# Linear attention and a gated feed-forward on one core: a new order of all steps

## The chip, the cores and the metric

The kernel runs on one core of a Trainium2 chip. The metric is device time in microseconds of one execution; lower is better. Before the change the median of three runs is 251.77 us (251.26 to 253.02).

## What is computed

The reference, cut to what matters:

```python
# q, k, v: 8 batches x 8 heads x 576 rows x 64, float32
phi = lambda x: np.where(x > 0, x, np.exp(x) - 1.0) + 1.0
kv  = einsum('bhsd,bhse->bhde', phi(k), v)
z   = sum(phi(k), axis=2)
x   = einsum('bhsd,bhde->bhse', phi(q), kv) / (einsum('bhsd,bhd->bhs', phi(q), z) + 1e-6)
x   = x.transpose(0, 2, 1, 3).reshape(4608, 512)
out = (((x @ w1) * (x @ w2)) @ w3) @ w_out        # w1, w2: 512x1024, w3: 1024x1024, w_out: 1024x512
```

## The kernel before

The kernel is a set of small steps (functions marked `@step`) and one string, ORDER, that lists every call of them. The scheduling is manual: each engine executes its own instructions in the order in which the string issues them, and an instruction that waits holds up everything behind it on its engine. A word such as `x:q,3,4,4` calls the step x with the arguments q, 3, 4, 4. A second string, GATES, adds waits between transfers: several of the loads on SP may not issue before the load of q of batch 1 has landed.

Of each batch, 512 of the 576 rows are worked on as one chunk of four row blocks (numbers 0 to 7); the remaining 64 rows of all batches together make a ninth chunk, number 8. Weights: `w3 @ w_out` is first multiplied out to `wf_sb` (steps w3t, w3c, wa, wf, wc), so that each chunk needs two matmul stages.

The steps, with their lines in the kernel before:

- Loads: `ld` (L119) brings one batch of q, k or v, 1 MB; `lr` and `lp` (L127, L135) the 64 rest rows of one batch or of two; `lw`, `lo`, `l3` (L144, L151, L159) the weights, cast to bf16, on POOL's queue. The last argument names the queue: s for SP, g for POOL. Loads of a 1 MB kind share five buffers.
- phi: `x` (L166, ACT) takes the exponential, `t` (L172, DVE) max and add, `m` (L180, DVE) the minimum of the two; `xr`, `tr`, `mr` (L194 to L212) do so for the rest rows. There is one buffer for the phi of q and one for that of k.
- `v` and `vr` (L217, L225) cast v to bf16, on DVE or ACT as the argument v or a says. There is one buffer for v.
- `kv` (L238, batches 0 and 1) and `kk` (L254, batches 2 to 7) multiply phi(k) by v on PE. `kc`, `kh`, `kg` copy the result from PSUM to `kvb`.
- phi(q) is transposed by PE (`qt`, copy `qc`) in batches 0 and 1, by a DMA on SP (`qd`, L299) after that.
- `na` (L311, PE) multiplies by kvb, `nd` (L317 to L319, three DVE instructions) divides and writes x; `qdr`, `nar`, `ndr` do so for the rest rows.
- x is transposed by PE (`xp`, L353, copy `xc`, L358) in batches 0 to 2, by a DMA on SP (`xd`, L363) in batches 3 to 7; `xdr` (L368) is that of the rest rows.
- `f` (L420, PE) makes one 128-row slice of x@w1 and x@w2, two PSUM banks of four matmuls each; `ac` (L434, ACT) copies the first to SBUF and `ab` (L439, DVE) multiplies. `fk` is a part of an f.
- `o` (L445, PE) makes one block of the output, `oc` (L451) copies it, `st` (L463) stores it. `ol` (L472 to L476) does so in two column halves on two engines and two queues.
- `warm` (L113) are matmuls on zeros.

PSUM has two pools: four banks shared by f, o, qt, xp, w3t and wf, and two pairs of banks shared by kv, kk, na, nar and wa. A new f therefore waits until the f two before it has been read by its ac and its ab.

Of the kernel before, what the change touches and what calls it, by code (L numbers as in the profile page):

```python
# [18 lines left out]
def kernel(  # L19
# [11 lines left out]
    nc = tc.nc  # L31
    B, H, S, D = q.shape
# [4 lines left out]
    NJ = 4  # L37
    R = S - NJ * P
    W = NJ * D
    E1 = D + 1  # L40
# [6 lines left out]
    ld = ctx.enter_context(tc.tile_pool(name="ld", bufs=5))  # L47
# [18 lines left out]
    vts = [wpool.tile([P, NJ, H, E1], BF16, name=f"vt{i}") for i in range(1)]  # L66
    vrz = wpool.tile([P, 2, H, E1], BF16)
# [179 lines left out]
    @step  # L247
    def kk(b, hp):
        o = got(ps, ("kk", b), at_ps, [P, 2, 512], F32, "at", "kvp")[:, 0]
        kj, kr, vt = ph["k", b], ph["kr", b // 2, 2], vts[b % len(vts)]  # L250
        for j in range(NJ + 1):
            for u in range(2):
                h = 2 * hp + u
                nc.tensor.matmul(o[u * D:(u + 1) * D, hp * E1:(hp + 1) * E1],  # L254
                                 kj[:, hp, j, u] if j < NJ else kr[:, h * D:(h + 1) * D],
                                 vt[:, j, h] if j < NJ else vrz[:, b % 2, h],
                                 start=(j == 0), stop=(j == NJ))
# [233 lines left out]
    xc:0,1,a xc:0,0,a ld:v,1,4,4,g fk:0,0,0,2 wc:6,v xp:0,2 xp:0,3 xc:0,2,a xc:0,3,v fk:0,0,2,1
    fk:0,0,3,1 ac:0,0,a ab:0,0 f:0,2 ac:0,2,a f:0,3 xr:k,0,1 tr:k,0,1 ab:0,2 ac:0,3,a mr:k,0,1 wf:7
    ab:0,3 f:0,5 wc:7,a vr:1,v ac:0,5,a f:0,7 ab:0,5 x:k,1,0,4 t:k,1,0,4 t:k,1,4,4 f:0,6 ac:0,7,a
    m:k,1,0,1 x:k,1,4,4 ab:0,7 m:k,1,0,0 ac:0,6,a m:k,1,4,2 f:0,4 m:k,1,4,3 x:q,1,4,4 lp:v,1,s t:q,1,0,4
    ab:0,6 ac:0,4,a ld:v,2,0,8,s f:0,1 x:q,1,0,4 t:q,1,4,4 ab:0,4 v:1,0,4,a m:q,1,0,1 m:q,1,4,2
    v:1,6,2,a m:q,1,4,3 kv:1,0 m:q,1,0,0 kv:1,1 ac:0,1,a lp:k,1,s kv:1,3 v:1,4,2,v kc:1,0,1,1,a qt:1,2,2
    kc:1,0,1,0,v kh:1,3,1,a kh:1,3,0,v ab:0,1 qt:1,0,2 qc:1,2,2,a kv:1,2 qc:1,0,2,v o:0,0 kh:1,2,0,a
    ld:k,2,0,8,s kh:1,2,1,a na:1,2 oc:0,0,a na:1,0 o:0,2 nd:1,2 st:0,0,g ld:q,2,0,8,s v:2,4,4,a vr:2,v
    nd:1,0 vr:3,a xp:1,2 na:1,1 oc:0,2,v v:2,0,4,a xp:1,0 na:1,3 nd:1,1 o:0,1 st:0,2,g xc:1,0,a
    ld:v,3,0,8,s nd:1,3 xc:1,2,a xp:1,1 oc:0,1,v xp:1,3 o:0,3 xc:1,1,a tr:k,1,2 st:0,1,g xr:k,1,2  # L500
    xc:1,3,a mr:k,1,2 x:k,2,4,4 t:k,2,0,4 f:1,7 lp:k,2,s t:k,2,4,4 oc:0,3,a m:k,2,4,2 ac:1,7,a m:k,2,4,3
    st:0,3,g x:k,2,0,4 ab:1,7 f:1,0 m:k,2,0,1 m:k,2,0,0 ac:1,0,a t:q,2,0,4 x:q,2,0,4 f:1,4 ab:1,0
    x:q,2,4,4 ld:q,3,0,8,s t:q,2,4,4 m:q,2,0,0 ac:1,4,a m:q,2,0,1 f:1,6 m:q,2,4,2 m:q,2,4,3 ab:1,4
    ac:1,6,a qd:2 f:1,2 ab:1,6 ac:1,2,a ab:1,2 f:1,1 ac:1,1,a f:1,3 x:q,3,4,4 t:q,3,0,4 lp:v,2,s ab:1,1
    ac:1,3,a tr:k,2,2 xr:k,2,2 t:q,3,4,4 f:1,5 ld:k,3,0,8,s x:q,3,0,4 ab:1,3 mr:k,2,2 ac:1,5,a kk:2,0
    kk:2,1 kk:2,2 kk:2,3 v:3,0,4,v ld:q,4,0,8,s ab:1,5 o:1,1 kg:2,0,a kg:2,1,a v:3,4,4,v m:q,3,0,0
    m:q,3,4,3 na:2,2 m:q,3,0,1 oc:1,1,a na:2,0 o:1,3 m:q,3,4,2 nd:2,0 st:1,1,g qd:3 nd:2,2 xp:2,0
    oc:1,3,a o:1,0 t:k,3,4,4 vr:4,a st:1,3,g t:k,3,0,4 x:k,3,4,4 xp:2,2 x:k,3,0,4 na:2,3 m:k,3,4,2
    na:2,1 m:k,3,4,3 o:1,2 nd:2,3 oc:1,0,a xc:2,2,a st:1,0,g m:k,3,0,0 xc:2,0,a nd:2,1 xp:2,3 x:q,4,0,4
    m:k,3,0,1 xp:2,1 t:q,4,0,4 xc:2,3,a kk:3,0 kk:3,1 kk:3,2 kk:3,3 oc:1,2,v xc:2,1,a ld:v,4,0,8,s  # L510
    kg:3,0,v st:1,2,g x:q,4,4,4 kg:3,1,v f:2,0 vr:5,v t:q,4,4,4 ac:2,0,a f:2,1 ab:2,0 ac:2,1,a m:q,4,4,2
    m:q,4,0,0 na:3,0 m:q,4,0,1 na:3,2 f:2,6 ab:2,1 nd:3,2 ac:2,6,a nd:3,0 f:2,4 v:4,4,4,a v:4,0,4,v
    ab:2,6 ac:2,4,a na:3,3 m:q,4,4,3 ld:k,4,0,8,s na:3,1 ab:2,4 f:2,7 lp:k,3,s nd:3,3 ac:2,7,a nd:3,1
    qd:4 f:2,3 ab:2,7 ac:2,3,a f:2,2 ab:2,3 ac:2,2,a t:k,4,0,4 x:k,4,4,4 f:2,5 t:k,4,4,4 x:k,4,0,4
    ab:2,2 ld:k,5,0,8,s xd:3 m:k,4,4,2 ac:2,5,a m:k,4,4,3 m:k,4,0,0 ab:2,5 o:2,2 m:k,4,0,1 xr:k,3,2
    tr:k,3,2 mr:k,3,2 oc:2,2,a kk:4,0 kk:4,1 kk:4,2 kk:4,3 o:2,3 kg:4,0,a st:2,2,g kg:4,1,a na:4,0
    oc:2,3,a na:4,3 o:2,1 nd:4,0 x:k,5,0,4 st:2,3,g nd:4,3 ld:q,5,0,8,s x:k,5,4,4 t:k,5,4,4 na:4,1
    na:4,2 oc:2,1,a o:2,0 nd:4,1 st:2,1,g m:k,5,4,2 nd:4,2 ld:v,5,0,8,s oc:2,0,a t:k,5,0,4 xd:4 st:2,0,g
    m:k,5,0,1 m:k,5,4,3 m:k,5,0,0 f:3,7 ac:3,7,a f:3,2 ab:3,7 ac:3,2,a x:q,5,4,4 t:q,5,0,4 f:3,4 ab:3,2
    x:q,5,0,4 t:q,5,4,4 f:3,3 m:q,5,4,2 ac:3,4,a m:q,5,0,1 ab:3,4 ac:3,3,a lp:v,3,s m:q,5,4,3 v:5,4,4,a  # L520
    m:q,5,0,0 f:3,0 ab:3,3 v:5,0,4,a qd:5 ac:3,0,a ab:3,0 kk:5,0 kk:5,1 kk:5,2 kk:5,3 f:3,6 kg:5,0,a
    kg:5,1,v ac:3,6,a ld:v,6,0,8,s f:4,6 ab:3,6 ac:4,6,a f:4,7 ab:4,6 vr:6,a vr:7,v ac:4,7,a f:4,3
    ab:4,7 ac:4,3,a na:5,2 na:5,0 ab:4,3 f:4,0 nd:5,2 v:6,0,4,a v:6,4,4,v ac:4,0,a lp:q,0,s na:5,3
    nd:5,0 f:4,4 ab:4,0 ld:q,6,0,8,s ac:4,4,a nd:5,3 ld:k,6,0,8,s f:4,1 ab:4,4 ac:4,1,a f:4,2
    ld:v,7,0,8,s ab:4,1 ac:4,2,a f:4,5 ab:4,2 x:q,6,4,4 t:q,6,4,4 t:q,6,0,4 x:q,6,0,4 f:3,1 m:q,6,4,2
    m:q,6,4,3 ac:4,5,a m:q,6,0,0 m:q,6,0,1 ac:3,1,a ab:4,5 o:4,0 qd:6 x:k,6,4,4 ab:3,1 t:k,6,0,4
    x:k,6,0,4 o:4,3 t:k,6,4,4 oc:4,0,a tr:q,0,2 xr:q,0,2 m:k,6,4,2 st:4,0,g m:k,6,4,3 ld:k,7,0,8,s
    m:k,6,0,1 oc:4,3,v o:4,2 mr:q,0,2 st:4,3,g m:k,6,0,0 oc:4,2,v qdr:0 kk:6,0 kk:6,1 kk:6,2 kk:6,3
    v:7,0,4,a o:4,1 st:4,2,g kg:6,1,v v:7,4,4,v kg:6,0,v na:5,1 oc:4,1,v f:3,5 nd:5,1 st:4,1,g ac:3,5,a
    xd:5 na:6,0 na:6,3 ab:3,5 o:3,1 nd:6,3 nd:6,0 o:3,3 oc:3,1,v x:k,7,0,4 t:k,7,4,4 st:3,1,g  # L530
    ld:q,7,0,8,s x:k,7,4,4 t:k,7,0,4 o:3,0 m:k,7,0,1 oc:3,3,a m:k,7,0,0 m:k,7,4,2 st:3,3,g m:k,7,4,3
    oc:3,0,a st:3,0,g kk:7,0 kk:7,1 kk:7,2 kk:7,3 o:3,2 kg:7,1,v kg:7,0,v na:6,2 oc:3,2,v na:6,1 f:5,7
    nd:6,1 st:3,2,g nd:6,2 ac:5,7,a f:5,6 xd:6 ab:5,7 ac:5,6,a nar:0 nar:1 ab:5,6 f:5,3 x:q,7,4,4
    t:q,7,4,4 lp:q,1,s x:q,7,0,4 ndr:1 f:5,2 m:q,7,4,3 ac:5,3,a m:q,7,4,2 ab:5,3 ac:5,2,a t:q,7,0,4
    f:5,4 m:q,7,0,0 ab:5,2 ac:5,4,a m:q,7,0,1 ndr:0 qd:7 f:6,1 ab:5,4 ac:6,1,a f:6,7 xdr:0 ab:6,1
    ac:6,7,a lp:q,2,s f:6,4 ab:6,7 lp:q,3,s ac:6,4,a f:6,2 ab:6,4 ac:6,2,a na:7,3 na:7,2 ab:6,2 f:6,6
    nd:7,2 xr:q,1,2 tr:q,1,2 ac:6,6,a mr:q,1,2 f:6,5 nd:7,3 qdr:1 ab:6,6 ac:6,5,a na:7,0 f:5,1 ab:6,5
    nd:7,0 ac:5,1,a f:6,0 ab:5,1 ac:6,0,a f:5,0 ab:6,0 xr:q,2,2 tr:q,2,2 ac:5,0,a mr:q,2,2 na:7,1 qdr:2
    f:5,5 ab:5,0 xr:q,3,2 tr:q,3,2 nd:7,1 ac:5,5,a nar:2 mr:q,3,2 xd:7 nar:3 ab:5,5 o:5,1 ndr:2 ndr:3
    o:5,0 qdr:3 oc:5,1,a st:5,1,g xdr:1 o:5,2 oc:5,0,a st:5,0,g o:5,3 oc:5,2,a st:5,2,g f:7,0 oc:5,3,a  # L540
# [49 lines left out]
```

## Time and profile before

| | |
|---|---|
| median of three runs | 251.77 us (251.26 to 253.02) |
| the profiled execution | 251.52 us, its span 249.7 us |
| PE busy | 236.0 us, 95% of the span |
| DVE / ACT / POOL busy | 164.1 / 122.9 / 36.4 us |
| DMA traffic | 50.10 MB, mean 201 GB/s |
| chain that ended last | PE 56%, DMA 32%, DVE 4%, issue 3%, ACT 2% |
| first f of batch 1 | PE, at 64.43 us |
| end of the last matmul | 246.3 us |

Engines: PE is the matmul engine, DVE the vector engine, ACT the scalar engine, POOL and SP issue transfers (SPq is SP's queue). A line of a timeline gives the start, the length, the engine, the line in the code, the operation, output<-inputs, how often it follows itself, and in brackets the idle time before it and what ended it. A line of the table by stretches gives the stretch, its length, the busy time (and number) of PE, of PE's weight loads, of DVE, ACT and POOL, the granted clock, the DMA share and GB/s. A line of the transfer view gives the tile, the queue, the number of issues, the size and the us from issue to landing.

### The profile page before, as it was taken

How to read it: one execution, taken by the hardware profiler on the slowest of the kernel's cores; microseconds unless marked ns; L12 is line 12 of the kernel's file. 1: busy time of each engine (PE TensorE's matmuls, PEld its weight loads, DVE VectorE, ACT ScalarE, POOL GpSimd, SP SyncE). 2: the span in 40 equal slices, each digit the busy share in tenths (PEclk: the TensorE clock that was granted, in tenths of full speed). 3: DMA queues.
4: the chain of work that ended last, by engine and by line, in shares of the span. 5: the costliest groups of instructions: out<-in, count | busy, mean ns of one | idle time of the engine just before them, and what ended most of it. 6: DMA issues, size and time to landing. Idle time of an engine off the chain costs nothing.

```text
span 249.7 us, 4327 instructions
## 1 busy us (share of the span) xinstructions
PE 236.0 (95%) x1620; PEld 122.9 (49%) x1636; DVE 164.1 (66%) x364; ACT 122.9 (49%) x190; POOL 36.4 (15%) x59
## 2 busy tenths in 40 slices
PE   6897889979999989999999999999999999999994
PEld 6654844445444555454444454544544444444442
DVE  7518764977868999959649889786775365042320
ACT  3409554776956774665744835153352332323211
POOL 8554720001100210011000032200001100000000
PEclk9999999999999999999999999999999999999999
DMA  6999999999998999999999699975409511210155
GB/s 120 204 265 348 214 198 294 314 248 319 336 240 227 281 294 287 211 248 351 189 265 335 182 248 260 291 175 107 105 12 128 179 22 21 91 38 29 55 144 153
DMA packets 69621, 50.10 MB, mean 201 GB/s; under 512 B 41312, under 2 KB 64096, under 8 KB 69600
## 3 DMA queue, kind: packets, MB, share of 16 engines
q1 hardware_dynamic: 60416, 31.86, 54.1%
q0 software_dynamic: 9040, 17.83, 28.0%
q8 instruction: 13, 0.21, 0.3%
q10 hardware_dynamic: 144, 0.13, 0.2%
q14 instruction: 8, 0.07, 0.1%
HBM read 38.80 MB, written 9.44 MB: 193 GB/s over the span
## 4 chain that ended last, share of the span: by engine, by line
PE 56%; DMA 32%; DVE 4%; issue 3%; ACT 2%; POOL 1%; SPq 0%; ACTq 0%; POOLq 0%; DVEq 0%
PE a_ps L420 17%; PE o_ps L445 17%; PE b_ps L420 17%; DMA v<-in_v_dram 13%; DMA q<-in_q_dram 9%; DMA w_sb<-in_moe_w_dram 4%; DMA wo<-in_moe_w_out_dram 3%; DMA k<-in_k_dram 3%; DVE xn L319 2%; PE nd L311 2%; PE kvp L254 1%; POOL w3b L159 1%; PE ndr L336 1%; PE o_ps L472 1%; ACT vt L217 1%
## 5 line engine op out<-in xcount | busy, mean ns | idle before, releaser
L420 PEld LDWEIGHTS <-w_sb 128*128 128x128 bf16 x576 | 55.6, 98 | 64.6 <-issue 0.6
L439 DVE TENSOR_TENSOR ab<-a_sb,b_ps 128x512 bf16<-128x512 f32 x72 | 49.0, 684 | 43.7 <-PE b_ps L420 40.1
L434 ACT COPY a_sb<-a_ps 128x512 f32<-128x512 f32 x72 | 42.1, 584 | 58.8 <-PE a_ps L420 52.7
L420 PE MATMUL a_ps<-xt,w_sb 128*128 128x512 bf16 x256 | 66.0, 379 | 0.5 <-ACT xt L358 0.5
L420 PE MATMUL b_ps<-xt,w_sb 128*128 128x512 bf16 x256 | 66.0, 379 | 0.0
L445 PE MATMUL o_ps<-wf_sb,ab 128*128 128x512 bf16 x267 | 62.9, 379 | 1.0 <-issue 0.2
L445 PEld LDWEIGHTS <-ab 128*128 128x128 bf16 x280 | 26.4, 98 | 30.3 <-DVE ab L439 1.2
L463 POOL DMA_DIRECT2D out_dram<-o_sb x24 | 14.5, 605 | 148.7 <-ACT o_sb L451 130.9
L451 ACT COPY o_sb<-o_ps 128x512 f32<-128x512 f32 x24 | 14.0, 585 | 34.1 <-PE o_ps L445 31.9
L319 DVE TENSOR_TENSOR xn<-nd,r 128x512 bf16<-128x512 f32 x32 | 22.1, 692 | 1.1
L166 ACT ACTIVATE e<-q 128x1024 bf16<-128x1024 f32 x16 | 16.5, 1056 | 1.8 <-DMA q<-in_q_dram 1.8
L166 ACT ACTIVATE e<-k 128x1024 bf16<-128x1024 f32 x16 | 16.4, 1058 | 0.9 <-DMA k<-in_k_dram 0.8
L451 DVE COPY o_sb<-o_ps 128x512 f32<-128x512 f32 x11 | 7.6, 687 | 8.0 <-PE o_ps L445 8.0
L217 ACT CAST vt<-v 128x1024 bf16<-128x1024 f32 (+1 forms) x11 | 10.2, 933 | 5.4 <-PE kvp L254 2.7
L180 DVE TENSOR_TENSOR k<-t,e 128x512 bf16<-128x512 bf16 x32 | 12.2, 418 | 0.4 <-ACT e L166 0.2
L172 DVE TENSOR_SCALAR t<-q 128x1024 bf16<-128x1024 f32 x16 | 10.9, 688 | 2.1 <-DMA q<-in_q_dram 2.1
L180 DVE TENSOR_TENSOR q<-t,e 128x512 bf16<-128x512 bf16 x32 | 11.9, 420 | 0.2
L311 PE MATMUL nd<-kvb,qt 128*128 128x130 bf16 x128 | 10.9, 220 | 0.9 <-DVE kvb L268 0.4
L172 DVE TENSOR_SCALAR t<-k 128x1024 bf16<-128x1024 f32 x16 | 10.5, 688 | 1.2 <-DMA k<-in_k_dram 1.1
L311 PEld LDWEIGHTS <-qt 128*128 128x128 bf16 x128 | 8.7, 98 | 4.9 <-DVE xn L319 1.0
L113 PE MATMUL warm<-zero 128*128 128x128 bf16 x116 | 9.2, 241 | 1.2 <-DVE zero L96 1.2
L318 DVE RECIPROCAL r<-r 128x8 f32<-128x8 f32 (+1 forms) x40 | 8.1, 202 | 1.4
(76 smaller groups left out, 191.6 us busy)
## 6 DMA issues: line engine op xcount, KB each, us to landing
v<-in_v_dram SPq DMA_DIRECT2D x6, 1024.0 KB, 9.8
k<-in_k_dram SPq DMA_DIRECT2D x6, 1024.0 KB, 8.7
q<-in_q_dram SPq DMA_DIRECT2D x6, 1024.0 KB, 9.2
out_dram<-o_sb POOLq DMA_DIRECT2D x24, 256.0 KB, 6.1
w3b<-in_moe_w_dram POOLq DMA_DIRECT2D x8, 256.0 KB, 8.1
out_dram<-o_sb SPq DMA_DIRECT2D x7, 256.0 KB, 2.3
v<-in_v_dram POOLq DMA_DIRECT2D x3, 512.0 KB, 18.9
out_dram<-o_sb SPq DMA_DIRECT2D x9, 128.0 KB, 2.4
```

The lines of the kernel that those rows point to most:

```text
L166: return nc.scalar.activation(out=e[:, 0:nh * W], in_=raw[n, b][:, h0 * W:(h0 + nh) * W], func=AF.Exp)
L172: nc.vector.tensor_scalar(out=d[:, 0:nh * W], in0=raw[n, b][:, h0 * W:(h0 + nh) * W], scalar1=0.0, scalar2=1.0, op0=ALU.max, op1=ALU.add)
L180: nc.vector.tensor_tensor(out=d[:, hp].rearrange("p j u d -> p u j d"), in0=ts[n, b, h0][:, s].rearrange("p (u j d) -> p u j d", u=2, j=NJ ...
L217: copy_of[eng](out=vts[b % len(vts)][:, :, h0:h0 + nh, 0:D], in_=raw["v", b].rearrange("p (h j d) -> p j h d", h=H, j=NJ)[:, :, h0:h0 + nh])
L311: nc.tensor.matmul(o[:, j // 2, (j % 2) * 256:(j % 2) * 256 + PW], sb["qt", b][:, hp, j * P:(j + 1) * P], kvb[b][:, hp].rearrange("p u e - ...
L319: nc.vector.tensor_tensor(out=dst, in0=o[:, :, :, 0:D], in1=r.unsqueeze(3).to_broadcast(list(r.shape) + [D]), op=ALU.mult)
L420: nc.tensor.matmul(o, w[:, kc, f * P:(f + 1) * P], xt_of(c)[:, :, kc, :], start=(kc == 0), stop=(kc == KC - 1))
L434: return copy_of[eng](out=d, in_=ps["a", c, f])
L439: nc.vector.tensor_mul(out=d[:, f, :], in0=sb["a", c, f], in1=ps["b", c, f])
L445: nc.tensor.matmul(d, sb["ab", c][:, f, m * P:(m + 1) * P], wf_sb[:, f, :], start=(f == 0), stop=(f == FC - 1))
L451: return copy_of[eng](out=d, in_=ps["o", c, m])
L463: queue_of[queue].dma_start(out=dst, in_=sb["o", c, m][r])
```

## The change

One step is rewritten: `kk`, which made one pair of heads per call, makes all four pairs in one call, with the same matmuls in the same sequence. ORDER is replaced by another order of the same steps, and one of the GATES stands at another place with the same content. The number of instructions of each kind stays the same, but for the engine that some copies run on (the last argument of kg, kh, kc, qc, xc, oc, v, vr, wc, w3c). What leads the search for an order, the planner's assumed length of DMA transposes and its trial with delayed transfers, is not part of the kernel's text.

On POOL's queue the first load of w3 stands ahead of the making of the identity; the rest of its loads keep their sequence. On SP's queue, up to the third transpose:

| before | after |
|---|---|
| lp v1, v2, lp k1, k2, q2, v3, lp k2, q3, transpose q2, lp v2, k3, q4, transpose q3 | k2, lp v1, lp k1, v2, q2, v3, k3, q3, transpose q2, lp v2, lp k2, q4, transpose q3 |

(lp v1 is the pair of rest rows that `lp:v,1` loads, v2 the 1 MB of `ld:v,2`.) Later on SP, `ld:k,7` moves from directly behind `qd:6` to behind the transposes `qd:7` and `xdr:1`, and `xd:7` moves to behind the first three of the stores that SP issues.

The diff, its order cut to the stretches that matter:

```diff
-    def kk(b, hp):
+    def kk(b):
         o = got(ps, ("kk", b), at_ps, [P, 2, 512], F32, "at", "kvp")[:, 0]
-        kj, kr, vt = ph["k", b], ph["kr", b // 2, 2], vts[b % len(vts)]
-        for j in range(NJ + 1):
-            for u in range(2):
-                h = 2 * hp + u
-                nc.tensor.matmul(o[u * D:(u + 1) * D, hp * E1:(hp + 1) * E1],
-                                 kj[:, hp, j, u] if j < NJ else kr[:, h * D:(h + 1) * D],
-                                 vt[:, j, h] if j < NJ else vrz[:, b % 2, h],
-                                 start=(j == 0), stop=(j == NJ))
+        kj, kr, vt = ph["k", b], ph["kr", b // 2, 2 if b > 1 else b], vts[b % len(vts)]
+        for h0 in range(0, H, 2):
+            for j in range(NJ + 1):
+                for h in (h0, h0 + 1):
+                    u = h % 2
+                    nc.tensor.matmul(o[u * D:(u + 1) * D, h0 // 2 * E1:(h0 // 2 + 1) * E1],
+                                     kj[:, h0 // 2, j, u] if j < NJ else kr[:, h * D:(h + 1) * D],
+                                     vt[:, j, h] if j < NJ else vrz[:, b % 2, h],
+                                     start=(j == 0), stop=(j == NJ))
...
-    const:0 lr:k,0,s const:8 warm:26,0 warm:18,9 const:1 lr:v,0,s const:6 zr:0,1 l3:0 const:2 const:9
-    l3:1 zr:0,0 const:11 l3:2 xr:k,0,0 tr:k,0,0 l3:3 const:5 lo:0,2 const:3 lo:2,2 lo:4,2 vr:0,a const:7
+    const:0 const:3 lr:k,0,s l3:0 lr:v,0,s const:1 l3:1 const:5 l3:2 warm:26,0 const:9 l3:3 xr:k,0,0
+    tr:k,0,0 lo:0,2 const:6 const:7 lo:2,2 zr:0,0 const:11 lo:4,2 warm:18,9 zr:0,1 mr:k,0,0 lo:6,2
...
-    w3t:4 wc:2,a wc:1,v w3t:5 wc:3,a l3:7 t:k,0,0,4 wc:0,a w3c:5,v x:k,0,0,4 wf:5 lw:0,0,256 w3c:4,a
-    t:k,0,4,4 m:k,0,0,0 x:k,0,4,4 m:k,0,0,1 lw:1,0,256 t:q,0,0,4 wf:4 x:q,0,0,4 wc:5,v m:k,0,4,3
+    l3:6 wc:3,a wc:1,v w3t:5 wc:0,a w3c:4,v wc:2,a w3c:5,v wf:4 l3:7 x:k,0,0,4 t:k,0,0,4 m:k,0,0,1
+    m:k,0,0,0 lw:0,0,256 x:k,0,4,4 wf:5 t:k,0,4,4 wc:4,v m:k,0,4,3 lw:1,0,256 x:q,0,0,4 m:k,0,4,2
...
-    kc:1,0,1,0,v kh:1,3,1,a kh:1,3,0,v ab:0,1 qt:1,0,2 qc:1,2,2,a kv:1,2 qc:1,0,2,v o:0,0 kh:1,2,0,a
-    ld:k,2,0,8,s kh:1,2,1,a na:1,2 oc:0,0,a na:1,0 o:0,2 nd:1,2 st:0,0,g ld:q,2,0,8,s v:2,4,4,a vr:2,v
-    nd:1,0 vr:3,a xp:1,2 na:1,1 oc:0,2,v v:2,0,4,a xp:1,0 na:1,3 nd:1,1 o:0,1 st:0,2,g xc:1,0,a
-    ld:v,3,0,8,s nd:1,3 xc:1,2,a xp:1,1 oc:0,1,v xp:1,3 o:0,3 xc:1,1,a tr:k,1,2 st:0,1,g xr:k,1,2
-    xc:1,3,a mr:k,1,2 x:k,2,4,4 t:k,2,0,4 f:1,7 lp:k,2,s t:k,2,4,4 oc:0,3,a m:k,2,4,2 ac:1,7,a m:k,2,4,3
+    kc:1,0,1,1,a kh:1,2,1,a kv:1,3 kh:1,2,0,a lp:k,1,s m:q,1,4,3 na:1,0 kh:1,3,1,v kh:1,3,0,v qt:1,2,2
+    ab:0,7 o:0,2 nd:1,0 qc:1,2,2,a ld:v,2,0,8,s x:k,2,0,4 t:k,2,4,4 o:0,0 oc:0,2,v ld:q,2,0,8,s
+    x:k,2,4,4 t:k,2,0,4 st:0,2,g m:k,2,0,1 xp:1,0 m:k,2,4,3 oc:0,0,a na:1,3 m:k,2,4,2 o:0,3 xc:1,0,a
+    m:k,2,0,0 ld:v,3,0,8,s st:0,0,g nd:1,3 vr:2,a vr:3,v na:1,2 xp:1,3 oc:0,3,v na:1,1 o:0,1 xc:1,3,a
+    nd:1,2 st:0,3,g xr:k,1,2 ld:k,3,0,8,s v:2,4,4,v xp:1,2 nd:1,1 oc:0,1,a st:0,1,g tr:k,1,2 xp:1,1
+    mr:k,1,2 xc:1,1,a xc:1,2,v v:2,0,4,v f:1,6 x:q,2,4,4 t:q,2,4,4 t:q,2,0,4 x:q,2,0,4 f:1,4
+    ld:q,3,0,8,s m:q,2,4,3 m:q,2,4,2 ac:1,6,a m:q,2,0,0 m:q,2,0,1 ac:1,4,a ab:1,6 f:1,3 qd:2 ab:1,4
+    ac:1,3,a f:1,7 ab:1,3 ac:1,7,a kk:2 ab:1,7 f:1,0 kg:2,1,a kg:2,0,v v:3,4,4,a t:k,3,4,4 t:k,3,0,4
+    ac:1,0,a f:1,1 v:3,0,4,v x:k,3,0,4 ab:1,0 x:k,3,4,4 m:k,3,0,1 m:k,3,0,0 f:1,5 lp:v,2,s x:q,3,4,4
+    m:k,3,4,2 m:k,3,4,3 t:q,3,0,4 ac:1,5,a kk:3 x:q,3,0,4 t:q,3,4,4 lp:k,2,s ab:1,5 kg:3,0,a ac:1,1,a
+    kg:3,1,v ab:1,1 f:1,2 ld:q,4,0,8,s ac:1,2,a m:q,3,4,2 na:2,1 m:q,3,0,0 na:2,3 m:q,3,4,3 ab:1,2 o:1,0
+    nd:2,3 m:q,3,0,1 nd:2,1 xp:2,3 qd:3 o:1,2 vr:5,a oc:1,0,v xc:2,3,a vr:4,v x:q,4,4,4 st:1,0,g
+    t:q,4,4,4 xp:2,1 na:2,2 o:1,1 t:q,4,0,4 x:q,4,0,4 tr:k,2,2 ld:k,4,0,8,s oc:1,2,v xc:2,1,a xr:k,2,2
+    nd:2,2 na:2,0 st:1,2,g o:1,3 oc:1,1,a nd:2,0 st:1,1,g xp:2,2 mr:k,2,2 oc:1,3,a xp:2,0 xc:2,2,v
+    xc:2,0,v st:1,3,g na:3,1 m:q,4,4,2 na:3,2 f:2,2 m:q,4,0,1 nd:3,2 ac:2,2,a m:q,4,0,0 f:2,4 nd:3,1
...
-    o:8,1 oc:8,3,a st:8,3,s o:8,0 oc:8,1,a st:8,1,s o:8,2 oc:8,0,v st:8,0,s o:7,0 oc:8,2,v st:8,2,s
-    oc:7,0,a st:7,0,s ol:7,3
+    ac:7,5,a o:8,1 ab:7,5 o:7,0 oc:8,1,v st:8,1,s ol:7,3 oc:7,0,v st:7,0,s o:7,1 o:8,0 oc:7,1,v st:7,1,s
+    o:8,3 oc:8,0,v st:8,0,s o:8,2 oc:8,3,a st:8,3,s o:7,2 oc:8,2,v st:8,2,s oc:7,2,a st:7,2,s
     """
```

## The prediction

> **What bounds the kernel now.** I read the page's busy times first, then the busy table by stretches, cut where the matrix engine's work changes character.
>
> ```profile
> span 249.7 us, 4327 instructions
> PE 236.0 (95%) x1620; PEld 122.9 (49%) x1636; DVE 164.1 (66%) x364; ACT 122.9 (49%) x190; POOL 36.4 (15%) x59
> ...
> DMA  6999999999998999999999699975409511210155
> ```
>
> ```profile
> 0.00:34.43 34.43, 28.57 (x293) 20.52 (x297) 21.33 (x50) 17.10 (x25) 21.84 (x35) 1.00 1.09 227
> 34.43:64.43 30.00, 27.62 (x180) 14.54 (x181) 20.99 (x47) 19.72 (x32) 1.66 (x3) 1.00 1.10 287
> 64.43:246.30 181.87, 179.81 (x1150) 87.88 (x1159) 121.79 (x268) 85.73 (x133) 12.86 (x21) 1.00 0.74 183
> 246.30:249.70 3.40, 0.00 (x0) 0.00 (x0) 0.00 (x0) 0.37 (x1) 0.00 (x0) 1.00 0.36 124
> ```
>
> PE is the bound in the third stretch (first column after the length: 179.81 of 181.87). In the first two the DMA share stands above 1, so PE waits for data. Next PE in order of time, for gaps and for the pace:
>
> ```profile
> 51.79 0.39 PE L238 MATMUL kvp<-vt,k 128*128 128x130 bf16 x4 [0.59 <-ACT vt L217]
> ...
> 62.70 1.89 PE L445 MATMUL o_ps<-wf_sb,ab 128*128 128x512 bf16 x7
> 64.43 1.03 PE L420 MATMUL a_ps<-xt,w_sb 128*128 128x512 bf16 x4
> 65.29 1.03 PE L420 MATMUL b_ps<-xt,w_sb 128*128 128x512 bf16 x4
> ...
> 88.70 0.40 PE L353 MATMUL xtp<-ident,xn 128*128 128x128 bf16 x4 [0.77 <-DVE xn L319]
> ```
>
> Four 512-column matmuls start every 0.864 us, so one costs 0.216, a step f or o (eight of them) 1.73. A 128-column one costs 0.057 (four in 0.227), a kk step 0.92 with its switches. Over the whole order that is 232.2 us, 6.6 of it warm-up: 225.6 of work. PE ends at 246.3, so 20.7 us are idle or warm-up: 18.5 before the first f:1 (45.9 of work in 64.43), 2.15 after it (179.7 in 181.87). Last, SP's queue and the transfer view of three of its loads (v2, q2, q3, asked at their issue):
>
> ```profile
> 52.18 1.21 SPq L119 DMA_DIRECT2D k<-in_k_dram  x1
> 53.55 3.32 SPq L119 DMA_DIRECT2D q<-in_q_dram  x1
> ...
> 64.44 1.96 SPq L119 DMA_DIRECT2D q<-in_q_dram  x1
> 71.04 4.37 SPq L299 DMA_TRANSPOSE qt<-q  x1
> 75.47 1.30 SPq L135 DMA_DIRECT2D v32r<-in_v_dram  x2
> ```
>
> ```profile
> v<-in_v_dram SPq DMA_DIRECT2D x1, 1024.0 KB, 8.3
> q<-in_q_dram SPq DMA_DIRECT2D x1, 1024.0 KB, 12.1
> q<-in_q_dram SPq DMA_DIRECT2D x1, 1024.0 KB, 11.2
> ```
>
> So v2 landed at 57.4, k2 (9.6 us, asked likewise) at 61.8, q2 at 65.6, q3 at 75.6: with four stores and two pairs of lp in between. Solving for these spacings: 2.95 us a load, 1.6 a pair of lp, 0.75 a store.
>
> **What the skill says.** The Trainium skill, "Perfetto Trace Analysis", section "DMA Instruction — HWDGE (DVE, Sync)": the profiled bar is the sequencer's time to make descriptors, not the movement. The trace agrees: the transpose bar above lasts 4.37 us and ends just before q3 landed, and nothing behind it on SP issues before. "DMA: Bandwidth & Descriptors", section "Issuing engines are not separate DMA queues": all queues run on the same 16 engines and interleave. Agreed: the 128 KB lp load issued at 31.8 while POOL's loads ran landed after 19.8 us (the longest v32r). "Perfetto Trace Analysis", section "Optimizing Scalar/DVE Operations": a profiled duration overlaps the next instruction in its acknowledgement half. Here the 0.69 us of an xn multiply lets the next start after 0.61; I use such steps below.
>
> **The change, part by part.** *kk as one step:* the four kk steps of a batch already stood together in all six batches, and PE has 3274 rows in both programs. Cost 0; there is no cover to lose. Everything else is order, so only idle can change, and after f:1 no more than 2.15 us can be won.
>
> *Head.* POOL's order differs by one swap: the first w3 load goes ahead of the identity (POOL spent 0.74 to 1.45 on it). That load starts 0.71 earlier; the next ones each wait for a landing eight back, in a stream the DMAs bound, so all of POOL's loads land about 0.7 earlier: q1 47.6 (48.3 before), the end of v1 51.7 (52.4). The vrz memset (0.93) ahead of others on DVE is hidden behind the wait for w3. If the stream does not follow, the cover is gone and the 0.7 is lost. Followed through PE: wa ends at 17.4 (18.1); wc:1 and w3c:4 stand first on DVE, so wf:4 starts at 19.0 and wf:5 ends at 22.5 (24.2); q0 and v0 land 0.7 earlier and na:0 begins at 28.8 (29.6); wf:6 runs from 31.15, wf:7 from 33.6 to 35.3, the last xt copy ends at 36.35. So f:0,2 starts at 36.4 with wf:7 done (before: at 37.2 one f was done and wf:7 not), 0.8 ahead, and the eight f:0 end at 50.2.
>
> *v1 to f:1.* The kv:1 steps wait for v1 (first half cast on DVE by 50.7, second half landed at 51.7). The last kv:1 runs at 53.2 to 53.5 (after two ACT casts and a kvb copy), then DVE is the chain from 53.75: two kvb copies 0.35, ab 0.6, nd 1.04, t(k2) 0.6, oc 0.6, t 0.6, four m 1.4, nd 1.04, vr 0.33, oc 0.6, nd 1.04, v2 cast 0.6, nd 1.04, tr, mr, xc 1.06: 10.9, hence f:1,6 at 64.75 against 64.43. So the 0.7 is spent, because t(k2), m(k2) and the v2 cast stand on DVE before the last nd, and PE waits at two xp steps (0.5 and 1.15). Step: +0.3. k2 must land before 55.8: on SP it is now first, behind the gate at q1, and from 47.6 with v1's last MB beside it I get 55.0. v2 must land by 62: 55.0 + 3.2 (two lp pairs) + 2.95 = 61.1. Known only to about 1 us.
>
> *f:1.* The order puts x:q,2 and t:q,2 ahead of ac:1,6 and ab:1,6; q2 at 65.5 just fits (PSUM pair wanted at 68.2, freed at 68.0). Then kk:2 moves from behind eight f to behind four, and kk:3 three f later, with x:k,3, x:q,3 and ac:1,1 in one row on ACT. From kk:2's end at 72.6: kvb copy 0.4 (from 72.8), v3 cast 1.0, ac 0.5, three exps 3.0, ac 0.5, exp 1.0, kvb copy 0.3, ac:1,1 0.55: 80.05. PE, with three f and a kk, is ready at 78.7; f:1,2 needs ac:1,1's bank: 1.45 us idle. k3 now precedes q3, so q3 lands at 55.0 + 3.2 + 5 x 2.95 + 4 stores 3.0 = 76.0, in time for its place on ACT at 76.7.
>
> *o:1 to f:2.* qd:2 ends its issue with q3, at 75.8; lp v2, lp k2 and q4 behind it give q4 at 85, before t:q,4 at 86. DVE then carries t:q,4 twice, tr, oc, two nd, mr, xc twice from 86.0 to 91.3: PE loses 0.45 at xp:2,0. Before lost 0.96 in the stretch f:1 to f:2 (0.77 of it shown). Step: 1.45 + 0.45 - 0.96 = +0.95.
>
> *Rest.* I laid every later load and transpose beside its consumer. On SP, lp v2 and lp k2 now stand behind qd:2, v5 behind xd:3, v6 behind qdr:0; each still lands 3 us or more ahead of its cast. k7, moved behind qd:7 and xdr:1, comes latest: issued about 181.5 after the second xnr transpose, 6.5 us alone on the queue as q7 had (154.8 to 161.7), 188 against a use at 189.6. xd:7 goes behind three stores on SP, five f:8 (8.6 us) cover it. Before idled 1.2 us here; one wait of 0.35 (kv for v5) has more cover now: -0.2.
>
> *Tail.* The split last tile (ol) moves forward; last is a whole o, copied on ACT (0.585 against 0.37), issued on SP (0.38 against 0.37), 256 KB landing in 2.0 against 1.5: with the start of the copy +0.75.
>
> **Sum:** 0.3 + 0.95 - 0.2 + 0.75 = +1.8: span 251.5. The profiled execution ran 251.52 (1.8 around its span), 0.25 under the median of 251.77; so 253.3 to 253.6, I say 253.4, +0.7%.
>
> Unknown costs and their ends: the lead of POOL's stream 0 to 0.8 (I take 0.7); landing of k2, v2, q2, q3 one us earlier (0, for ACT and DVE bind) to 3 us later (+3, nearly one for one at f:1,2); DVE's row before f:1 -0.9 to +1; k7 0 to +2; the rest -0.5 to +1.5.
>
> **Rivals.** *B, a late load:* q3 (behind k3 now) lands late, and x:q,3 holds ac:1,5 and ac:1,1 on ACT and PE behind them. Free until 76.7, then a us per us; it makes the kernel slower by over 1% (254.3) from 77.5 on, and at 79.0 gives 255.7. For: the DMA row is at 9 there and k3 is an extra load before it. Against: two lp pairs went behind it. *C, stalls covered:* DVE reaches the last nd 0.9 earlier and ACT's row costs 0.9 less, the head's lead stays: 251.6. For: 0.7 of lead is real work of POOL. Against: both rows are sums of measured steps. *D, a gain over 1%:* needs 249.2, that is PE done 3.2 us before 246.3 though the longer tail stays; all 2.15 idle after f:1 and 2 us more ahead of it would have to go. *E, nothing moves:* PE is 99% busy after 64.43, so order could be neutral, 251.8; counted with C.
>
> **Chances.** Forecast 0.44 (252.0 to 254.5, a tenth of it above 254.3), B 0.34, C and E 0.17, D 0.05. About 1% is what a measurement of this kernel can tell from no change. Slower by over 1%: 0.34 + 0.04 = 0.38; within: 0.40 + 0.17 = 0.57; faster 0.05. The range leaves out D, the best of C and the worst of B: 250.3 to 257.0.
>
> **What will show it.** First w3 load issued at 0.74, v1 landed near 51.7, f:0,2 at 36.4; f:1,6 at 64.75 with xp waiting on DVE xn; a PE gap of 1 to 1.5 us near 79 named after ACT a_sb; q3 landed near 76; no gap over 0.5 after 92; 4.2 us between PE's end and the span's. I am wrong if f:1 starts before 64, if no gap stands near 79, or if one over 1 us stands after 92.

## The result, and the profile after

The changed kernel takes 253.17 us (median of 15 runs, 252.53 to 254.34), the kernel before beside it 252.09: a ratio of 1.0047, 95% interval 1.0026 to 1.0069. The profiled execution ran 252.88 us with a span of 251.1, against 251.52 and 249.7 before. One execution is one draw: those of the kernel before spread here from 251.20 to 253.35, so what follows splits the difference of two executions. The page of the kernel after:

```profile
span 251.1 us, 4331 instructions
PE 237.4 (95%) x1636; PEld 123.6 (49%) x1636; DVE 170.6 (68%) x374; ACT 115.6 (46%) x180; POOL 35.2 (14%) x59
...
DMA  6999999999998699889969769998992045000155
```

Some 6 to 7 us of copies and casts went from ACT to DVE. The table by stretches, cut at the same four times as before:

```profile
0.00:34.43 34.43, 29.18 (x288) 21.08 (x289) 21.25 (x49) 14.89 (x22) 21.19 (x35) 1.00 1.08 225
34.43:64.43 30.00, 28.16 (x186) 14.72 (x184) 23.96 (x53) 18.76 (x31) 1.65 (x3) 1.00 1.11 290
64.43:246.30 181.87, 179.41 (x1162) 87.75 (x1163) 125.42 (x275) 81.40 (x127) 12.38 (x21) 1.00 0.72 182
246.30:249.70 3.40, 0.66 (x4) 0.10 (x1) 0.00 (x0) 0.59 (x1) 0.00 (x0) 1.00 0.63 168
```

PE (first column after the length) is the bound of the third stretch in both kernels, and ends 0.66 us later. PE's timeline shows where it stands still now:

```profile
65.53 0.40 PE L354 MATMUL xtp<-ident,xn 128*128 128x128 bf16 x4 [1.24 <-DVE xn L320]
65.77 0.38 PE L421 MATMUL a_ps<-xt,w_sb 128*128 128x512 bf16 x1
66.60 0.81 PE L421 MATMUL a_ps<-xt,w_sb 128*128 128x512 bf16 x3 [0.46 <-ACT xt L359]
...
80.19 1.04 PE L421 MATMUL a_ps<-xt,w_sb 128*128 128x512 bf16 x4
...
83.70 1.47 PE L446 MATMUL o_ps<-wf_sb,ab 128*128 128x512 bf16 x6 [0.73 <-DVE ab L440]
...
92.32 1.04 PE L421 MATMUL a_ps<-xt,w_sb 128*128 128x512 bf16 x4 [0.17 <-DVE xt L359]
```

The first f of batch 1 starts at 65.77 with one matmul, waits for a copy and is whole from 66.60: as if it had started at 66.38, against 64.43. The gap forecast near 79 is not there: f:1,2 follows its kk at 80.19. Behind 92.32 no gap is left.

I take a gap as the time from one matmul's start to the next's, less its own 0.216 us (0.057 for a narrow one); the switches to and from kk, 0.09 us each in both kernels, are left out. The trace of the kernel before lacks 16 matmul records (1620 against 1636); where one is missing, no gap is counted. Then the difference splits so:

| | before | after | difference | forecast |
|---|---|---|---|---|
| first f of batch 1, as if whole | 64.43 | 66.38 | +1.95 | +0.3 |
| gaps from there to 93 us | 1.11 | 1.25 | +0.14 | +0.95 |
| gaps behind 93 us | 1.4 | 0 | -1.4 | -0.2 |
| end of PE to end of span | 3.4 | 4.1 | +0.7 | +0.75 |
| sum | | | +1.4 (spans: +1.4) | +1.8 |

The third row can be checked by a second sum: both kernels do the same PE work from that f on, and PE needs 181.84 us for it before and 180.58 after, 1.26 less. One of the gaps of before that are gone is this wait:

```profile
122.88 0.32 PE L254 MATMUL kvp<-vt,k 128*64 128x65 bf16 x8 [0.35 <-ACT vt L217]
```

The time came out near the forecast (medians +1.1, spans +1.4, forecast +1.8), but three of its four terms were wrong and cancelled.

### The profile page after: what moved, and what is told of

Same layout as the page of the kernel before. It is cut to its first block, busy times and chain, and to the rows that moved or that the text cites. A ratio compares the mean times of both kernels' runs of the same rounds, so it can differ in the third digit from the quotient of the medians.

```text
span 251.1 us, 4331 instructions
## 1 busy us (share of the span) xinstructions
PE 237.4 (95%) x1636; PEld 123.6 (49%) x1636; DVE 170.6 (68%) x374; ACT 115.6 (46%) x180; POOL 35.2 (14%) x59
## 3 DMA queue, kind: packets, MB, share of 16 engines
q1 hardware_dynamic: 60416, 31.86, 53.2%
## 4 chain that ended last, share of the span: by engine, by line
PE 76%; DVE 11%; ACT 5%; DMA 3%; issue 3%; POOL 1%; DVEq 0%; POOLq 0%
PE a_ps L421 23%; PE b_ps L421 22%; PE o_ps L446 19%; DMA wo<-in_moe_w_out_dram 3%; PE wa L394 3%; DVE xn L320 2%; PE nd L312 2%; DVE k L180 2%; DVE t L172 2%; PE kvp L255 2%; PE wf_ps L409 1%; ACT e L166 1%; PE kvp L238 1%; ACT a_sb L435 1%; DVE q L180 1%
## 5 line engine op out<-in xcount | busy, mean ns | idle before, releaser
L446 PE MATMUL o_ps<-wf_sb,ab 128*128 128x512 bf16 x280 | 64.4, 379 | 0.7 <-DVE ab L440 0.7
L452 ACT COPY o_sb<-o_ps 128x512 f32<-128x512 f32 x18 | 10.5, 585 | 29.9 <-PE o_ps L446 29.8
L452 DVE COPY o_sb<-o_ps 128x512 f32<-128x512 f32 x17 | 11.7, 687 | 11.1 <-PE o_ps L446 11.0
L312 PE MATMUL nd<-kvb,qt 128*128 128x130 bf16 x128 | 11.5, 220 | 0.5 <-ACT kvb L280 0.5
L172 DVE TENSOR_SCALAR t<-k 128x1024 bf16<-128x1024 f32 x16 | 11.1, 696 | 0.0
L217 ACT CAST vt<-v 128x1024 bf16<-128x1024 f32 (+1 forms) x11 | 9.6, 895 | 0.4 <-DMA v<-in_v_dram 0.4
L113 PEld LDWEIGHTS <-zero 128*128 128x128 bf16 x116 | 8.9, 118 | 1.4 <-DVE zero L96 1.2
```

What stands on the lines that cost most here:

```text
L113: nc.tensor.matmul(t[:, 0:P], zero[:, 0:P], zero[:, 0:P], start=True, stop=True)
L172: nc.vector.tensor_scalar(out=d[:, 0:nh * W], in0=raw[n, b][:, h0 * W:(h0 + nh) * W], scalar1=0.0, scalar2=1.0, op0=ALU.max, op1=ALU.add)
L312: nc.tensor.matmul(o[:, j // 2, (j % 2) * 256:(j % 2) * 256 + PW], sb["qt", b][:, hp, j * P:(j + 1) * P], kvb[b][:, hp].rearrange("p u e - ...
L446: nc.tensor.matmul(d, sb["ab", c][:, f, m * P:(m + 1) * P], wf_sb[:, f, :], start=(f == 0), stop=(f == FC - 1))
L452: return copy_of[eng](out=d, in_=ps["o", c, m])
```

## The experiments

Each time below is the median of 6 to 22 executions, and the ratio is to the kernel before, run beside it; edits are moves of words in ORDER, `-` where a word stood, `+` where it stands. The kernel after is the start unless another is named.

**ident_first.** `- l3:0 lr:v,0,s const:1` becomes `+ const:1 l3:0 lr:v,0,s`: POOL's swap undone.

> The changed kernel with one word moved: the identity is made on POOL ahead of the first w3 load again, as before the change. Theory (the swap cost the head time): in the changed kernel POOL's first load started at 1.26 and the second only at 2.47, so w3's second load landed at 8.21 instead of 7.41; with the swap undone the whole stream comes 0.75 us earlier, f:0,2 starts near 37.3 instead of 38.1, the first f of batch 1 near 65.7 instead of 66.4, and the span falls by 0.6 to 0.8 us. Rival (the head's lateness is DVE's or PE's own): the loads come earlier but f:0,2 and f of batch 1 stay within 0.2 us and the time does not move.

252.75 us, ratio 1.0040 (1.0021 to 1.0058), span 251.0: a miss. POOL's timeline of the kernel after:

```profile
1.26 0.68 POOL L159 DMA_DIRECT2D w3b<-in_moe_w_dram  x1 [0.81 <-POOLq L573]
1.93 0.22 POOL masks.py:197 MEMSET ident<- 128x128 bf16 x1
2.23 0.29 POOL masks.py:199 TENSOR_SCALAR_AFFINE_SELECT ident<-ident 128x128 bf16<-128x128 bf16 x1
2.47 1.63 POOL L159 DMA_DIRECT2D w3b<-in_moe_w_dram  x3
```

and of ident_first:

```profile
0.74 0.20 POOL masks.py:197 MEMSET ident<- 128x128 bf16 x1 [0.29 <-POOLq L573]
1.02 0.29 POOL masks.py:199 TENSOR_SCALAR_AFFINE_SELECT ident<-ident 128x128 bf16<-128x128 bf16 x1
1.45 2.29 POOL L159 DMA_DIRECT2D w3b<-in_moe_w_dram  x4
```

With the load first, POOL stands idle for 0.81 us ahead of it, so it gains 0.19 and not 0.71; the identity then delays the second load by 0.35. With the swap undone the second load of w3 lands at 7.51 instead of 8.21, but k of batch 0 at 20.32 (20.14 in the kernel after): the stream as a whole does not come earlier. f:0,2 starts at 37.53 instead of 38.09, and the first kv:1 at 52.28 instead of 52.40. The 0.56 us are absorbed on DVE: there the rest rows of v of batch 1, which land at 45.32, are waited for (1.34 us), and the cast of v that PE waits for begins at 51.53 instead of 51.65.

**w3_first_in_before.** The same swap made in the kernel before: `- const:1 lr:v,0,s const:6 zr:0,1 l3:0` becomes `+ l3:0 const:1 lr:v,0,s const:6 zr:0,1`.

> The kernel before with one move: the first load of w3 ahead of the identity on POOL, as the change has it. Theory (the swap costs, because the first load waits at the head of POOL all the same, 1.26 in the changed kernel, and the identity then stands between the first and the second load): first load issued at 1.26 instead of 1.45, second at 2.47 instead of 2.12, so the first w3 block lands earlier and all loads from the second on 0.3 to 0.4 us later, k of batch 0 at 19.8 to 20.2; end of the kernel 0 to 0.6 us later, because the end of v of batch 1 may hide it. Rival (the prediction: the swap advances the whole stream by 0.7): first load at 0.74 and k at 18.7. Rival (the later stream in the changed kernel has another cause, such as the vector engine's row or the instruction fetches): k lands at 19.4 as before, time unchanged.

252.16 us, ratio 1.0001 (0.9981 to 1.0022), span 250.7. Loads issued at 1.26 and 2.47, k of batch 0 at 20.70. Over 22 runs the time is that of the kernel before, so the swap costs nothing that can be measured. In this trace the first f of batch 1 comes 1.6 us late, at 66.03, but something else stands in it too: PE waited 2.06 us up to 22.08, and from 22.9 to 26.3 its granted clock was 0.50. There its lag behind the kernel before grew from 1.15 to 2.77 us. How far the stream moves by itself shows in before_head_after_rest (below), whose start is that of the kernel before: k at 19.91 instead of 19.40, f of batch 1 at 65.14 instead of 64.43. So some 0.7 of the +1.95 above may be such scatter (an estimate from this one pair), though in the five traces that share this part of the order (after, ident_first, both split_tile_last, q3_behind_transpose) the f is always whole from 66.45 to 66.80.

**v2_cast_late.** `- ld:k,3,0,8,s v:2,4,4,v xp:1,2` and `+ xc:1,2,v v:2,4,4,v v:2,0,4,v`: one cast on DVE behind the last division of chunk 1.

> The changed kernel with the first cast of v of batch 2 on DVE moved behind the last division of batch 1. Theory (DVE's row before the first f of batch 1 is the chain there): the last division starts 0.6 us earlier, the 1.24 us wait of PE on DVE xn shrinks to about 0.6, the first f of batch 1 runs from about 65.8 instead of 66.4, and the time falls by 0.3 to 0.6 us. Rival (the row of ACT and DVE between kk:2 and f:1,2 takes it back): PE is earlier at f:1 but waits 0.5 us or more near f:1,2, and the time stays.

252.84 us, ratio 1.0039 (1.0020 to 1.0059), span 250.6. The wait for xn falls from 1.24 to 0.64 and f:1,6 is whole from 65.97: the cast's 0.6 us, as the row of DVE predicts. f:2 starts 0.47 earlier.

**dve_row_cleared.** The four `m:k,2,...` go to the same place as well.

> The changed kernel with the four minima of k of batch 2 and the first cast of v of batch 2 moved from between the divisions of chunk 1 to behind them. Theory (VectorE's row of 10.9 us before the first f of batch 1 is what sets its start): that f runs whole from about 64.7 instead of 66.6, the waits for xn shrink from 1.5 us to under 0.5. How much stays at the end depends on q of batch 4: it lands at 86.2 and its use moves to 85, so 0.7 to 1.9 us remain; span 249.2 to 250.4, ratio to before 0.998 to 1.003. Rival (what holds the first f is PE's own chain of transposes and copies, or the minima are missed at kk of batch 2): f moves less than 0.7, or a new gap of over 1 us stands at 71 to 74.

252.68 us, ratio 1.0041 (1.0020 to 1.0063), span 250.5. PE's timeline:

```profile
64.09 0.40 PE L354 MATMUL xtp<-ident,xn 128*128 128x128 bf16 x4 [0.23 <-DVE xn L320]
64.33 0.38 PE L421 MATMUL a_ps<-xt,w_sb 128*128 128x512 bf16 x1
65.17 0.81 PE L421 MATMUL a_ps<-xt,w_sb 128*128 128x512 bf16 x3 [0.46 <-ACT xt L359]
...
70.97 1.02 PE L421 MATMUL a_ps<-xt,w_sb 128*128 128x512 bf16 x4 [0.69 <-DVE ab L440]
```

The f is whole 1.43 us earlier, so DVE's row did set it. (About 2.0 us of work left the row; 0.47 of that became a new wait of DVE for PE, at 59.55.) 0.85 of the gain is lost at once: ab of that f now stands behind the moved minima, and the third f wants its bank. f:2 starts 0.6 earlier (91.73).

**q3_behind_transpose.** `ld:q,3,0,8,s` goes from behind `f:1,4` to behind `qd:2`, so that on SP it waits for the transpose: rival B by force.

> The changed kernel with the load of q of batch 3 moved on SP from ahead of the first DMA transpose to behind it. Theory B of the prediction as a mechanism (a load behind its place on ACT costs PE one for one): q3 lands near 80 instead of 76.3, its exponential stood at 78.1 on ACT, so ac:1,1 and f:1,2 come about 2 us later than 80.2, and the time rises by 1.5 to 2.5 us. Rival (slack further on takes it up): the gap near f:1,2 shows, but the time rises by less than 1 us.

255.28 us, ratio 1.0137 (1.0108 to 1.0166), span 253.4: 2.3 more than after. q3 lands at 80.4 instead of 76.3; in the kernel after its exponential ran at 78.11, so 2.3 of the 4.1 us exceed the slack. PE, and ACT in the same stretch:

```profile
80.25 0.20 PE L255 MATMUL kvp<-vrz,kr 128*64 128x65 bf16 x2
82.02 1.02 PE L421 MATMUL a_ps<-xt,w_sb 128*128 128x512 bf16 x4 [1.57 <-ACT a_sb L435]
```

```profile
80.44 1.06 ACT L166 ACTIVATE e<-q 128x1024 bf16<-128x1024 f32 x1 [2.04 <-DMA q<-in_q_dram]
81.40 0.57 ACT L435 COPY a_sb<-a_ps 128x512 f32<-128x512 f32 x1
81.87 1.06 ACT L166 ACTIVATE e<-q 128x1024 bf16<-128x1024 f32 x1
82.83 0.36 ACT L263 CAST kvb<-kvp 64x260 bf16<-64x260 f32 x1
83.08 1.06 ACT L435 COPY a_sb<-a_ps 128x512 f32<-128x512 f32 x2
```

f:1,2 starts at 82.02, when the copy of 81.40 ends. By its place in the order (between the two exponentials of q3) that is ac:1,5; ac:1,1 comes at 83.08. So f:1,2 writes into the banks of f:1,5, which ORDER gives back first, and not into those of f:1,1. Here, then, a new f does not wait for the f two before it, as the section on the kernel before has it.

**split_tile_last.** `ol:7,3` and `o:7,2` with its copy and store change places.

> The changed kernel with the split output tile last again (ol:7,3 at the end, o:7,2 in its old place). Theory: the time from the end of the last matmul to the end of the span falls from 4.1 to 3.4 us, nothing else moves, so the time falls by 0.6 to 0.7 us. Rival (the stores queued on SP hold up the last one, whatever its size): 4.0 us or more stay and the time does not move.

253.54 us, ratio 1.0057 (1.0032 to 1.0081), span 251.9: a miss. From PE's end to the span's it is 4.2 us as in the kernel after. The store of SP's half was issued at 247.99, 0.7 after its copy: o:8,2 now stood directly ahead, whose store is issued in two pieces (246.79 to 247.90). What landed last was ACT's half: issued at 248.17, right behind its copy, it took 2.61 us to land, against 1.87 in the kernel before. The trace also had q of batch 4 at 87.7 (86.2) and lost 0.7 there.

**split_tile_last_before_tail.** `ol:7,3` goes to the very end, behind `o:7,2`.

> The changed kernel with the split tile moved behind the last whole tile of chunk 7, so that the end is that of the kernel before: chunk 8, then a whole tile with one store, then the split one. Theory (the earlier try gave nothing because a tile of chunk 8, whose store is issued in two pieces of 0.5 us each, stood directly ahead of the split one, and its bytes were still moving): 3.4 us from the end of the last matmul to the end of the span instead of 4.1, time 0.6 to 0.7 us under the changed kernel, ratio to before about 1.002. Rival (the longer tail has to do with where chunk 8 stands, not with the split): 4.1 us again, no change.

252.81 us, ratio 1.0033 (1.0015 to 1.0050), span 250.2. The end of this kernel, without PE's weight loads:

```profile
244.90 1.91 PE L473 MATMUL o_ps<-wf_sb,ab 128*128 128x256 bf16 x16
245.10 0.59 ACT L452 COPY o_sb<-o_ps 128x512 f32<-128x512 f32 x1 [2.87 <-PE o_ps L446]
245.98 0.42 DVE L475 COPY o_sb<-o_ps 128x256 f32<-128x256 f32 x1 [1.91 <-PE o_ps L473]
246.43 0.34 SPq L477 DMA_DIRECT2D out_dram<-o_sb  x1
246.85 0.37 ACT L475 COPY o_sb<-o_ps 128x256 f32<-128x256 f32 x1 [1.16 <-PE o_ps L473]
247.25 0.37 ACTq L477 DMA_DIRECT2D out_dram<-o_sb  x1
```

PE ends at 246.81, the span 3.4 later: the tail of before, and the 0.7 is back in the trace. The medians show 0.0014 of the ratio (0.35 us), with intervals that overlap.

**before_head_after_rest.** ORDER of before up to `f:2,0` (its kk as one step), then every word of the new order that was not yet used.

> Order of the kernel before up to the first f of batch 2, order of the changed kernel from there, with its tail. Theory (the new order is better only behind the first f of batch 2, where it has no gap and the kernel before has 1.3 us of them, and worse ahead of it and in the tail): span 249.7 - 1.3 + 0.7 = 249.1, ratio about 0.998. Rival (the gaps behind 92 come from loads that depend on how the first part ran, so they return): span 250.4, ratio 1.003.

255.62 us, ratio 1.0136 (1.0098 to 1.0174), span 254.8: neither came. PE, and SP ahead of it:

```profile
93.05 1.05 PE L312 MATMUL nd<-kvb,qt 128*128 128x130 bf16 x8 [2.50 <-DMA qt<-q]
```

```profile
77.77 0.56 SPq L119 DMA_DIRECT2D k<-in_k_dram  x1
78.44 0.52 SPq L119 DMA_DIRECT2D q<-in_q_dram  x1
82.99 5.21 SPq L300 DMA_TRANSPOSE qt<-q  x1
```

The new order multiplies by the transpose of q3 earlier; in the new order only q4 stands ahead of it on SP, here k3 and q4 do, and its bar ends when q4 lands (88.0), so that it lands at 93.0 instead of 89.9. Behind that wait PE also ran at half its pace: from 93.0 to 96.4 the granted clock was 0.50 and the 512-column matmuls started every 0.43 us, which costs another 1.7 us (an estimate: half of the 3.4). Two gaps of 0.46 and 0.40 follow by 103 us. Behind 103, however, there is none, where the kernel before loses the 1.4 us of the table (0.27 near 105, 0.25 near 111, 0.42 near 122 and 0.20 near 188 are the longest). PE comes there 3.7 us later than in the kernel after, which leaves the loads more time; but no trace of the new order has a gap there, so the gapless rest belongs to that order.

**row_cleared_ab_early** and **row_shared_with_act**. The first is dve_row_cleared with `ac:1,6,a` and `ab:1,6` moved ahead of minima of q2, and the tail of split_tile_last_before_tail. The second also gives `oc:1,0`, `oc:1,2`, `xc:2,2` to ACT (`,v` becomes `,a`) and puts both `t:q,4` behind `nd:2,0`.

> The changed kernel with three moves at once: the minima and the first cast of batch 2 behind the divisions (as in dve_row_cleared), the multiplication ab of the first f of batch 1 ahead of two of the four minima of q of batch 2, and the split tile last behind a whole tile of chunk 7. Theory (of the 1.4 us that clearing VectorE's row won at the first f, 0.85 went because the third f waited for ab of the first; behind it VectorE is busy without a pause from kk of batch 2 to f:2, so that a kk earlier by 1.3 moves f:2 earlier by as much, up to the landing of q of batch 4): f whole from 65.2, no gap over 0.3 at 71, f:2 at 91.2 to 91.6 against 92.3, 3.6 us from the last matmul's start to the end; span 249.2 to 249.6, ratio to before 0.998 to 1.001. Rival (the gain at the first f is given back at the next wait whatever is moved): f:2 at 91.7 or later, span 250.0 or more, ratio 1.002 or more.

> As row_cleared_ab_early, and three copies (two of the output, one of a transposed x) between o:1 and f:2 on ScalarE instead of VectorE, and the max and add of q of batch 4 behind the divisions of chunk 2. Theory (from kk of batch 2 to f:2 VectorE is the bound; 1.8 us of copies leave it, and its wait for q of batch 4 goes behind what PE needs): f:2 at 89.8 to 90.6, so 0.7 to 1.4 us under the other; a wait for the transpose of q of batch 3, which lands at 89.8, may take up to 0.9 of it; span 248.3 to 249.2, ratio to before 0.994 to 0.999. Rival (PE's own work or ScalarE's row takes over at once): f:2 no more than 0.4 earlier, ratio as the other's.

First: 252.72 us, ratio 1.0016 (0.9994 to 1.0038), span 251.0; the gap at 71 is down to 0.18, the f whole 12.7 us after the first kv:1 (14.2 in after), but this trace came to that kv 1.3 late. Second: 252.14 us, ratio 1.0001 (0.9974 to 1.0027), span 249.9; f whole from 64.81, f:2 at 91.93, not 90. Its gaps: 1.12 at 69.2, because the exponential of q2 (landed at 66.55) held the copy of the first f on ACT, 0.89 at 83.0, 0.57 at 91.9.

**row_shared_waits_moved.** Those three waits put behind other work: `ac:1,6,a` ahead of `x:q,2,4,4`, `ab:1,6` ahead of `t:q,2,4,4`, three `m:q,3` behind `nd:2,3`, both `t:q,4` behind `xc:2,0,v`, `na:3,1 na:3,2` and the division `nd:3,2` behind `f:2,4`.

> As row_shared_with_act, with the four waits that its trace still shows between f:1 and f:2 each put behind other work: the copy and the multiplication of the first f of batch 1 ahead of the exponential of q of batch 2 (its load landed 1.5 us later than PE could start, and held that copy), three minima of q of batch 3 behind the last ab of chunk 1, the max and add of q of batch 4 behind the last copy of xt, and the two multiplications by kvb of batch 3 behind the first two f of chunk 2. Theory (each of these waits costs its own length, 1.1, 0.9 and 0.5 us, as VectorE and ScalarE have room now): f:2 at 89 to 90 instead of 91.9, no gap over 0.3 at 69, 83 and 92, span 247.7 to 248.6, ratio to before 0.991 to 0.997. Rival (the loads pace this stretch: q of batches 2, 3 and 4 land 10 us apart whatever the order of the steps, so the time comes back as a wait for the transpose of q of batch 3 or for k of batch 4): new gaps behind 90 of 1 us or more, span 249.3 or more, ratio 0.998 or more.

252.88 us, ratio 1.0033 (1.0013 to 1.0053), span 250.4. The gaps at 69 and 83 are gone, f:2 starts at 90.88, and new waits stand in ACT's and DVE's timelines:

```profile
77.50 1.06 ACT L166 ACTIVATE e<-q 128x1024 bf16<-128x1024 f32 x1 [0.95 <-DMA q<-in_q_dram]
```

```profile
74.62 1.29 DVE L172 TENSOR_SCALAR t<-k 128x1024 bf16<-128x1024 f32 x2 [1.22 <-DMA k<-in_k_dram]
...
98.22 0.68 DVE L440 TENSOR_TENSOR ab<-a_sb,b_ps 128x512 bf16<-128x512 f32 x1
```

k3 and q3 land at 74.5 and 77.5, and the engines are there first. Nine gaps of 0.13 to 0.69 between 76 and 102, 3.0 us in all, take the place of the three (2.58); the two near 100 came, by their place in the order, because ab (98.22) stands behind the divisions that were moved there. The rival was nearer. None of the versions is measurably faster than the kernel before.

## Why the prediction was right, and where it was not

**The bound, kk as one step, the tail:** right. kk takes 0.76 us from first matmul to the next step in both kernels (89.03 to 89.79 before, 73.38 to 74.14 after). With its two switches that is 0.85 and not 0.92, so the idle time behind f:1 was 2.5 us in the kernel before and not 2.15. The tail measured +0.7 for +0.75, and goes, in the trace, when the split tile is last behind a tile of chunk 7.

**Head:** "That load starts 0.71 earlier ... all of POOL's loads land about 0.7 earlier" failed. It started 0.19 earlier and the others later; k of batch 0 landed at 20.14 (19.40 before), f:0,2 started at 38.09 instead of 36.4. Undoing the swap gives back 0.56 of these 1.7 us; where the rest comes from stays open. v1 landed at 51.23 (51.7 forecast) all the same, perhaps because lp v1 no longer stood beside it on SP, which no run tests. As ident_first shows, 0.56 us at f:0,2 are worth 0.1 at kv:1.

**v1 to f:1:** the mechanism was right, the size not (+1.95 for +0.3). The two xp waits were 0.24 and 1.24 (0.5 and 1.15). The row on DVE began with the kvb copies at 55.15 instead of 53.75, since the eight f:0 ended at 51.9 (50.2), the cast of v at 52.3 (50.7), and the last kv:1 began at 54.43 (53.2). The row took 11.45 us to f whole instead of 10.9. Shortening it moves f: by 0.6 for 0.6 of work, by 1.4 for about 2.0.

**f:1:** "f:1,2 needs ac:1,1's bank: 1.45 us idle" failed, and the measured gap is zero. The bank was that of f:1,5, whose copy comes about 1.7 us earlier on ACT. The loads on SP landed near their forecasts: k2 at 54.9 (55.0), v2 at 60.8 (61.1), q2 at 65.1 (65.5), q3 at 76.3 (76.0); q4 was later, at 86.2 (85). So rival B did not come; its price, a us per us once the slack is used, shows in q3_behind_transpose: 2.3 us behind its place, 2.3 more at the end.

**o:1 to f:2:** 0.45 was forecast at xp:2,0; what came was 0.89 at o:1, where the last ab stands behind three minima of q3, and 0.33 at f:2. I had costed the row behind that ab, not the ab in it. With the forecast gap at f:1,2 missing, the step is +0.14 for +0.95.

**Rest:** -1.4 for -0.2. I counted one gap of the kernel before (0.35) and took the others to stay; all went. before_head_after_rest shows that this belongs to the new order behind 103 us.

So errors of +1.65, -0.8 and -1.2 nearly cancelled, and that the sum came out close is luck. By its own test ("I am wrong if ... no gap stands near 79") the step at f:1,2 was wrong. With DVE's row cleared, more copies on ACT and the tail of before, row_shared_with_act is back at a ratio of 1.0001 (0.9974 to 1.0027); which of the three brings how much, the medians do not resolve. What stays open is how much of the +1.95 is the order and how much scatter of the loads (0.7 between two traces with the same start). The gains in the traces of the mended versions (0.5 to 1.2 us) appear only in part in their medians; in part this is because the traced executions were 0.4 to 0.8 us faster than the medians of their versions, that of the kernel after only 0.3.

## What to carry to other kernels

A row of work on one engine can set when a step on another starts, but what a shorter row wins is kept only as far as the next row or load lets it through: of the 1.43 us that dve_row_cleared won at the first f, 0.6 were left at f:2, and in row_shared_waits_moved the three waits that were mended came back within 30 us as others. A new order moves many such waits at once, so cost the many small gaps of the old order too, not just the new ones. Ask which bank or buffer a step really takes: here, of two that were in use, it was the one given back first.

## What the runs showed of the hardware

The first DMA on POOL was issued at 1.26 us with nothing ahead of it, in ten traces, and at 1.45 behind the making of the identity: 0.57 us of other work fitted into that wait for a price of 0.19. The landings agree: the first load at 5.14 in the kernel after and 6.06 in ident_first, the second at 8.21 and 7.51. The same load in nearly the same queue moved by 3.5 us between traces (q2 landed between 63.3 and 66.8), so a place in the order with less slack than that isn't safe here. Of the first four transposes of q in each trace, those issued on SP before the load ahead of them had landed kept their bar up to about that landing (76.09 for q3 at 76.34, 88.20 for q4 at 88.04, at most 1.5 us behind it). Their bars lasted 1.8 to 7.1 us; those of transposes issued after that landing lasted 1.3 to 1.9. The granted clock fell to 0.50 for 3.4 us in two traces, both times behind a long wait of PE (2.06 us in w3_first_in_before, 2.50 in before_head_after_rest), and the 512-column matmuls then started every 0.43 us instead of 0.216; a wait of 1.98 us, at 8.47 in row_cleared_ab_early, was not followed by it.
